# Sink-window attention, cosine FFN and top-1 experts on one core: masks, first pair and routing constants in another order

## The chip, the cores and the metric

One NeuronCore of a Trainium2 chip runs the whole program. It has a tensor engine (PE, with its weight loads as PEld), VectorE (DVE), ScalarE (ACT), GpSimd (POOL) and SyncE (SP); 16 DMA engines move data between HBM and SBUF. The metric is the device time of one execution in microseconds; of several runs the median is given.

## The reference

```python
# attention: q, k, v are 4 x 8 x 768 x 64; 4 sink keys, a window of 128
scores = scale * np.matmul(q, k.transpose(0, 1, 3, 2))
keep = is_sink | in_window            # key < n_sink, or 0 <= row - key < window
scores = np.where(keep, scores, -1e9)
a = softmax(scores); x = a @ v        # -> 3072 tokens x 512
# feed-forward, 512 -> 2048 -> 512
h = x @ w_in; x = (h * np.cos(h)) @ w_out
# eight experts, one per token
logits = x @ w_gate + modality_bias[modality_id]
e_idx = np.argmax(logits, axis=1); gate_w = softmax(logits)[e_idx]
out[mask] = gate_w * (np.maximum(x[mask] @ w1[e], 0.0) @ w2[e])
```

`n_sink` and `window` are inputs that the kernel reads at run time; the weights of the feed-forward layer come as 64-bit floats.

## The kernel before

**Tiling.** Work is cut into eight halves of 384 tokens (one batch element has two). In each half, attention goes by four pairs of heads; then the FFN works on the half as one tile, over 16 blocks of 128 hidden units. The code weaves the FFN of one half into the attention of the next; in the first half there is attention alone, and beside it the conversion of the FFN's weights (`conv_gen`, three raw buffers of 512 KB): a scaled copy on ScalarE (`cv_h`, line 261), bit operations on VectorE, a rounded copy on ScalarE (line 299) and a difference on VectorE.

**One pair of heads** (`attn_front`). Queries and keys are loaded by four DMAs on SyncE (lines 424, 425; every second pair uses other tiles, `ld_x`), transposed on the tensor engine into `pq` and `pk` (lines 444, 454), and evicted by ScalarE into `qT` and `kT` (lines 450, 468); VectorE copies the sink keys. `mid` makes six score tiles `ps` (line 136 through `mm`), takes their masked minimum on VectorE (line 502, writing `Pb` and `mx`; it needs `masks`) and the exponential on ScalarE (line 518). `rest` transposes the probabilities (`pt`, lines 555, 556), multiplies with the values (`po`), scales by the sums (`pf`, a product with the identity matrix `ident`) and writes `xT`. The values' loads are `load_v` (lines 432, 433).

**Set-up** (lines 842 to 943). The two limits are loaded into `rt` (lines 849, 850), converted (`rf`, line 852) and clamped into `lim`. From them come the test `bad` (is the window or the number of sinks beyond what the fast path handles?) and, with two iotas of GpSimd, the three masks. After that stand constants that only the routing of tokens needs, much later: `sides`, `tri`, `ones`, `bias_all`, `tok1`, `e8`, `base`, `inv`, with three loads (`wg`, `mb`, `mid`, lines 916 to 920; `mid` is 3072 items of 8 bytes).

**The general path** (line 160) is a branch that every engine takes part in: it reads `bad_i` into a register (line 943) and jumps over a block that would redo the attention for any limits. It isn't taken here.

**Order of issue.** Each engine works through its own queue in order. The order within it isn't the order of the code: a scheduler draws it up when the program is built, from the code's order, the dependencies and its own costs; the trace shows the result (`cv_h` stands before `qT` on ScalarE, though the code has it behind). An If is one unit to it, but other instructions may be moved past it.

**The expert stage** walks over pages of 256 tokens; a page with more than 128 filled rows takes one arm of an If, others the other (`full`, lines 1330 on). A branch hint, line 1327, tells the tensor engine alone which arm comes.

Of the kernel before, what the change touches and what calls it, by code (L numbers as in the profile page):

```python
# [11 lines left out]
F32 = DT.float32  # L12
# [8 lines left out]
P = 128  # L21
# [35 lines left out]
CONV_A = 0.2  # L57
CONV_LEAD = 8


@with_exitstack
def kernel(
# [92 lines left out]
    def general_attention():  # L155
# [3 lines left out]
        NB = S // P  # L159
        with tc.If(bad_r > 0):  # L160
            def room(tag, n):
# [90 lines left out]
    def conv_out(cpool, f):  # L252
        r = cpool.tile([P, 2 * DM], I32, name="cv_out", tag="cv_raw", bufs=CVB)
        SP.dma_start(out=r, in_=w_out[f * P:(f + 1) * P, :])
        return r

    def conv_bits(cpool, raw):
        w = raw.rearrange("p (n t) -> p n t", t=2)
        lo, hi = w[:, :, 0], w[:, :, 1]
        h = cpool.tile([P, 512], F32, name="cv_h", bufs=2)  # L260
        ACT.activation(out=h, in_=hi.bitcast(F32), func=AF.Copy, scale=REBASE)
        h = h.bitcast(I32)
        a = cpool.tile([P, 512], I32, name="cv_a", bufs=2)
# [131 lines left out]
    def attn_front(hb, pr):  # L395
# [66 lines left out]
        if stack:  # L462
            ACT.activation(out=kT[0][:, 0:nblk, 0:P], in_=pk3[:, 0:nblk, :], func=AF.Copy)
            tt(DVE, kT[1][:, 0:nblk, 0:P], pk3[:, 0:nblk, :], kT[0][:, 0:nblk, 0:P].bitcast(F32), ALU.subtract)
            for i in range(2):
                DVE.tensor_copy(kT[i][:, 0:nblk - 1, P:SEG], ks[:, pr, i:i + 1, :].to_broadcast([P, nblk - 1, NS]))
        else:
            ACT.activation(out=kT[0][:, 0:nblk, 0:P], in_=pk3[:, 0:nblk, :], func=AF.Copy)  # L468
            src = pk3[:, 0:1, 0:NS] if half == 0 else ks[:, pr, 0:1, :]
            DVE.tensor_copy(kT[0][:, 0:nblk - 1, P:SEG], src.to_broadcast([P, nblk - 1, NS]))  # L470
# [394 lines left out]
    win_c = lim[:, 1:2]  # L865
    bad = tmpc.tile([P, 2], F32, name="bad")
    ts(DVE, bad[:, 0:1], ns_c, float(NS), ALU.is_gt)
    ts(DVE, bad[:, 1:2], win_c, float(P), ALU.is_gt)
    tt(DVE, bad[:, 0:1], bad[:, 0:1], bad[:, 1:2], ALU.add)
    ts(DVE, bad[:, 1:2], win_c, 1.0, ALU.is_lt)  # L870
    tt(DVE, bad[:, 0:1], bad[:, 0:1], bad[:, 1:2], ALU.add)
    bad_i = const.tile([P, 1], I32, name="bad_i")
    DVE.tensor_copy(bad_i, bad[:, 0:1])


    iota_i = tmpc.tile([P, NV], I32, name="iota_i")
    POOL.iota(iota_i, pattern=[[1, NV]], base=0, channel_multiplier=0)
    iota_f = const.tile([P, NV], F32, name="iota_f")
    DVE.tensor_copy(iota_f, iota_i)
    prow_i = tmpc.tile([P, 1], I32, name="prow_i")  # L880
    POOL.iota(prow_i, pattern=[[0, 1]], base=0, channel_multiplier=1)
    cols2 = const.tile([P, 2], F32, name="cols2")
    prow, half_pi = cols2[:, 0:1], cols2[:, 1:2]
    DVE.tensor_copy(prow, prow_i)

    masks = const.tile([P, 3, W3], BF16, name="masks")
    rel = tmpc.tile([P, P], F32, name="rel")
    sk = tmpc.tile([P, P], F32, name="sk")
    mw = tmpc.tile([P, P], F32, name="mw")
    ts(DVE, rel, iota_f[:, 0:P], prow, ALU.subtract, -1.0, ALU.mult)  # L890
    ts(DVE, sk, iota_f[:, 0:P], ns_c, ALU.is_lt)
    POOL.memset(masks, 0.0)

    ts(DVE, mw, rel, win_c, ALU.is_lt)
# [8 lines left out]
    DVE.tensor_copy(masks[:, 2, P:SEG], sk[:, 0:NS])  # L903
    ts(DVE, masks, masks, -1.0, ALU.add, -NEG / SCALE, ALU.mult)

    sides = const.tile([P, 2, P], BF16, name="sides")
    ts(DVE, sides[:, 0], rel, 0.0, ALU.is_gt)
    ts(DVE, sides[:, 1], rel, 0.0, ALU.is_le)
    tri = const.tile([P, P], BF16, name="tri")
    ones = const.tile([P, P], BF16, name="ones")  # L910
    ts(DVE, tri, rel, 0.0, ALU.is_lt)
    DVE.memset(ones, 1.0)
    DVE.memset(half_pi, HALF_PI)

    wg = const.tile([P, KD, NE], F32, name="wg")
    SP.dma_start(out=wg, in_=w_gate.rearrange("(c p) e -> p c e", p=P))
    mb = tmpc.tile([P, 2, NE], F32, name="mb")
    SP.dma_start(out=mb, in_=mod_bias.rearrange("(o m) e -> o (m e)", o=1).partition_broadcast(P).squeeze(1).rearrange("p (m e) -> p m e", m=2))
    mid = tmpc.tile([P, NTI, 2], I32, name="mid")
    SP.dma_start(out=mid, in_=modality.rearrange("(t p) w -> p t w", p=P))  # L920
    bias_all = const.tile([P, NTI, NE], F32, name="bias_all")
    btmp = tmpc.tile([P, NTI, NE], F32, name="btmp", tag="iota_i")
    m01 = tmpc.tile([P, NTI, 2], F32, name="m01")
    DVE.tensor_copy(m01[:, :, 1], mid[:, :, 0])
    ts(DVE, m01[:, :, 0], m01[:, :, 1], -1.0, ALU.mult, 1.0, ALU.add)
    b3 = [P, NTI, NE]
    tt(DVE, bias_all, m01[:, :, 0:1].to_broadcast(b3), mb[:, 0:1, :].to_broadcast(b3), ALU.mult)
    tt(DVE, btmp, m01[:, :, 1:2].to_broadcast(b3), mb[:, 1:2, :].to_broadcast(b3), ALU.mult)
    tt(DVE, bias_all, bias_all, btmp, ALU.add)


    tok1 = const.tile([P, NTI], F32, name="tok1")
    ts(DVE, tok1, iota_f[:, 0:NTI], float(P), ALU.mult, 1.0, ALU.add)
    ts(DVE, tok1, tok1, prow, ALU.add)
    e8 = const.tile([P, NE], F32, name="e8")
    ts(DVE, e8, iota_f[:, 0:NE], -1.0, ALU.mult, float(NE), ALU.add)
    base = const.tile([P, NE], F32, name="base")
    DVE.memset(base, 0.0)
    inv = const.tile([P, NV + 2], F32, name="inv")
    DVE.memset(inv, 0.0)  # L940

    tmps.close()
    bad_r = nc.values_load(bad_i[0:1, 0:1], min_val=0, max_val=3)


    next(conv)
    for _ in first:
        pass
    fronts[0, 0][0]()
    mids.add((0, 0))  # L950
    for _ in fronts[0, 0][1]():
        pass
    general_attention()
    conv_done = 1

    def conv_to(n):
        nonlocal conv_done
        while conv_done < n:
            conv_done += 1
            next(conv, None)  # L960

    for n_, _ in enumerate(attn_half(0)):
        conv_to(int(CONV_A * n_))
    def more_wi():
        assert conv_done < 4 * NE1
# [48 lines left out]

    ET = mybir.EngineType
    ALLE = (ET.Pool, ET.Activation, ET.PE, ET.DVE, ET.SP)
# [274 lines left out]
    def run(T):  # L1291
# [102 lines left out]
```

## Time and profile before

| | |
|---|---|
| median of 3 runs | 1143.38 us (1141.84 to 1145.58) |
| the profiled execution | 1143.94 us, of which the span 1142.2 us |
| tensor engine busy | 1103.6 us |
| VectorE busy | 678.3 us |
| ScalarE busy | 602.5 us |
| GpSimd busy | 224.5 us |
| DMA | 113.40 MB, mean 99 GB/s |

The span is the time from the first to the last instruction in the trace; what lies around it is the rest of the measured time. A busy tensor engine is not one at its peak, since matmuls are pipelined. Rows of a timeline give the start in us from the span's start, the length in us, the engine, the line, the operation, what is written from what, and in brackets how long the engine had been idle and what ended that. "SPq" is the issue of a DMA by SyncE, not the transfer.

### The profile page before, as it was taken

How to read it: one execution, taken by the hardware profiler on the slowest of the kernel's cores; microseconds unless marked ns; L12 is line 12 of the kernel's file. 1: busy time of each engine (PE TensorE's matmuls, PEld its weight loads, DVE VectorE, ACT ScalarE, POOL GpSimd, SP SyncE). 2: the span in 40 equal slices, each digit the busy share in tenths (PEclk: the TensorE clock that was granted, in tenths of full speed). 3: DMA queues.
4: the chain of work that ended last, by engine and by line, in shares of the span. 5: the costliest groups of instructions: out<-in, count | busy, mean ns of one | idle time of the engine just before them, and what ended most of it. 6: DMA issues, size and time to landing. Idle time of an engine off the chain costs nothing.

```text
span 1142.2 us, 20840 instructions
## 1 busy us (share of the span) xinstructions
PE 1103.6 (97%) x6624; PEld 928.0 (81%) x6624; DVE 678.3 (59%) x2126; ACT 602.5 (53%) x1239; POOL 224.5 (20%) x273
## 2 busy tenths in 40 slices
PE   5989999999999999999999999999999999999995
PEld 3667777888888878888888879999889998899984
DVE  6778888666876766776676774746742125522210
ACT  5878887656665566665657553434322225422221
POOL 1232224211111111111111111322121211221110
PEclk9999999999999999999999999999999999999998
DMA  6567665422332322323233223633151115111110
GB/s 150 151 197 196 195 195 158 109 73 68 95 74 76 105 72 64 108 70 75 63 104 79 62 75 102 230 93 89 60 203 40 57 58 184 41 58 39 40 43 23
DMA packets 136083, 113.40 MB, mean 99 GB/s; under 512 B 95727, under 2 KB 103919, under 8 KB 135920
## 3 DMA queue, kind: packets, MB, share of 16 engines
q1 hardware_dynamic: 131600, 97.87, 30.3%
q0 software_dynamic: 4320, 13.65, 3.7%
q8 instruction: 66, 1.08, 0.4%
q14 instruction: 97, 0.79, 0.2%
HBM read 151.06 MB, written 19.67 MB: 149 GB/s over the span
## 4 chain that ended last, share of the span: by engine, by line
PE 85%; DVE 5%; DMA 5%; ACT 2%; issue 1%; POOL 1%; SPq 0%; DVEq 0%; POOLq 0%; ACTq 0%
PE hp L136 23%; PE y L626 22%; PE m_h L136 10%; PE m_y L136 10%; PE ps L136 5%; PE po L136 5%; DMA out_dram<-m_ot,m_ids 3%; DMA cv_in<-in_moe_w_in_dram 1%; PE pl L754 1%; PE pq L444 1%; PE pt L546 1%; PE yT L743 1%; PE pk L454 1%; PE m_a L1093 1%; PE mh L136 1%
## 5 line engine op out<-in xcount | busy, mean ns | idle before, releaser
L148 POOL TENSOR_TENSOR g_l<-ch,g_h 128x384 fp32r<-128x384 f32 x128 | 132.4, 1035 | 558.2 <-ACT g_h L698 435.4
L136 PE MATMUL hp<-xT_h,wi_h 128*128 128x384 f32 x512 | 188.3, 368 | 2.7 <-DVE ch L148 2.7
L136 PE MATMUL hp<-xT_h,wi_l 128*128 128x384 f32 x512 | 174.5, 341 | 0.0
L136 PE MATMUL hp<-xT_l,wi_h 128*128 128x384 f32 x512 | 174.0, 340 | 0.0
L626 PE MATMUL y<-wo,g_h 128*128 128x512 f32 x384 | 158.6, 414 | 0.0
L626 PE MATMUL y<-wo_l,g_h 128*128 128x512 f32 x384 | 155.6, 405 | 0.0
L626 PE MATMUL y<-wo,g_l 128*128 128x512 f32 x384 | 154.1, 401 | 0.2 <-POOL g_l L148 0.2
L688 ACT ACTIVATE ch<-ch,cols 128x384 f32<-128x384 f32 x128 | 78.7, 616 | 116.6 <-DVE ch L145 116.0
L136 PE MATMUL m_y<-wi_h,hT 128*128 128x512 f32 x416 | 132.5, 393 | 0.7 <-ACT m_ot L1135 0.6
L145 DVE SCALAR_TENSOR_TENSOR hT<-m_h,hT 128x256 fp32r<-128x256 f32 x88 | 37.3, 424 | 151.0 <-ACTq L1287 102.4
L136 PEld LDWEIGHTS hp<-xT_h,wi_h 128*128 128x128 f32 x512 | 96.7, 189 | 18.1 <-issue 7.2
L142 DVE TENSOR_SCALAR ch<-hp 128x384 int32<-128x384 f32 x128 | 70.9, 554 | 59.1 <-PE hp L136 46.3
L698 ACT ACTIVATE g_h<-ch 128x384 fp32r<-128x384 f32 x128 | 66.4, 520 | 67.8 <-DVE ch L148 46.0
L136 PEld LDWEIGHTS hp<-xT_l,wi_h 128*128 128x128 f32 x512 | 97.0, 189 | 3.7 <-issue 0.2
L136 PEld LDWEIGHTS hp<-xT_h,wi_l 128*128 128x128 f32 x512 | 96.7, 189 | 1.2 <-issue 0.9
L148 DVE TENSOR_TENSOR ch<-ch,hp 128x384 f32<-128x384 f32 x128 | 70.4, 550 | 39.9 <-ACT ch L688 39.5
L136 PEld LDWEIGHTS m_y<-wi_h,hT 128*128 128x128 f32 x416 | 78.1, 188 | 17.0 <-issue 1.0
L518 ACT ACTIVATE Pb<-Pb,mx 128x272 f32<-128x272 f32 (+1 forms) x168 | 82.9, 494 | 10.9 <-DVE mx L502 10.0
L626 PEld LDWEIGHTS y<-wo,g_l 128*128 128x128 f32 x384 | 72.2, 188 | 14.8 <-POOL g_l L148 0.8
L626 PEld LDWEIGHTS y<-wo,g_h 128*128 128x128 f32 x384 | 72.4, 189 | 13.8 <-issue 3.3
L502 DVE CUSTOM_DVE_ANT_0 Pb<-ps,masks 128x272 f32<-128x272 f32 (+1 forms) x168 | 63.7, 411 | 31.7 <-PE ps L136 31.2
L136 PE MATMUL ps<-kT,qT 64*128 64x272 f32 (+1 forms) x504 | 72.6, 350 | 8.9 <-ACT kT L468 7.0
(276 smaller groups left out, 2236.0 us busy)
## 6 DMA issues: line engine op xcount, KB each, us to landing
rw<-in_moe_w_dram SPq DMA_DIRECT2D x112, 512.0 KB
wo_l<-wl_scr SPq DMA_DIRECT2D x122, 256.0 KB
cv_in<-in_moe_w_in_dram SPq DMA_DIRECT2D x16, 512.0 KB
cv_out<-in_moe_w_out_dram SPq DMA_DIRECT2D x16, 512.0 KB
y_scr<-yt SPq DMA_DIRECT2D x24, 256.5 KB
xT_h<-xg_h SPq DMA_DIRECT2D x32, 192.0 KB
xT_l<-xg_l SPq DMA_DIRECT2D x32, 192.0 KB
qn<-in_q_dram SPq DMA_DIRECT2D x56, 96.0 KB
```

What stands on the lines that cost most here:

```text
L136: PE.matmul(o, l, r, start=start, stop=stop)
L142: e.tensor_scalar(out=o, in0=i, scalar1=s1, scalar2=s2, op0=op0, op1=op1)
L145: e.scalar_tensor_tensor(out=o, in0=i0, scalar=s, in1=i1, op0=op0, op1=op1)
L148: e.tensor_tensor(out=o, in0=a, in1=b, op=op)
L444: PE.transpose(pq[:, t * P:(t + 1) * P], qn[:, t].rearrange("p j d -> p (j d)"), ident)
L454: PE.transpose(pk[:, t * P:(t + 1) * P], kn[:, t].rearrange("p j d -> p (j d)"), ident)
L502: DVE.tensor_tensor_reduce(out=Pb[t][j][:, c0:c1], in0=ps[j][:, 0:w], in1=masks[:, min(half * NQ + t, 2), c0:c1], scale=-SCALE, scalar=3.0 ...
L518: ACT.activation(out=Pb[t][j][:, c0:c1], in_=Pb[t][j][:, c0:c1], func=AF.Exp, scale=-1.0, bias=mx[:, i:i + 1], accum_out=sm[:, i:i + 1])
L546: PE.transpose(pt2[:, j * P:(j + 1) * P], Pb[t][j][:, SEG:W3], ident)
L626: i = PE.matmul(o, l, r, start=start, stop=stop)
L688: ACT.activation(out=ch, in_=ch, func=AF.Sin, scale=TWO_PI, bias=half_pi)
L698: ACT.activation(out=gh, in_=ch, func=AF.Copy)
```

## The change

The set-up is put in another order. The limits' DMAs go to ScalarE's queue; iotas and mask fill come first on GpSimd; the masks' instructions on VectorE are tied into one order; the test follows them, with `max` for the additions; the test's register is read there and a branch hint with the label of the general path is placed for four engines. Only then the first pair's loads, transposes and scores stand in the code, VectorE's part behind the masks; between transposes and scores ten products of the identity with itself go into a PSUM bank that nobody reads. The first conversion on ScalarE is tied behind the eviction of the first keys. The router's three loads stand behind the general path, and the router's constants at the twelfth step of the first half's attention. In the expert stage the hint goes to ScalarE and VectorE too. Values computed are the same.

```diff
+RCONST = 12
+WARM = 10
...
-        with tc.If(bad_r > 0):
+        with tc.If(bad_r > 0, preferred_fallthrough_block=True, label="general"):
...
+    nosync = mybir.DependencyInfo(mybir.DependencyClass.NoSync, mybir.DependencyReason.DATA)
+    front_act = []
...
-        ACT.activation(out=h, in_=hi.bitcast(F32), func=AF.Copy, scale=REBASE)
+        i_ = ACT.activation(out=h, in_=hi.bitcast(F32), func=AF.Copy, scale=REBASE)
+        if front_act:
+            tc.add_manual_dep(i_.ins, front_act[-1].ins.name, nosync, reason="behind the first keys")
+            front_act.clear()
...
+            i_ = ACT.activation(out=kT[0][:, 0:nblk, 0:P], in_=pk3[:, 0:nblk, :], func=AF.Copy)
+            if hb == 0 and pr == 0:
+                front_act.append(i_)
...
-    first = attn_front(0, 0)
-    next(first)
-    next(first)
...
-    SP.dma_start(out=rt[:, 0:2], in_=n_sink.partition_broadcast(P).squeeze(1))
-    SP.dma_start(out=rt[:, 2:4], in_=window.partition_broadcast(P).squeeze(1))
+    ACT.dma_start(out=rt[:, 0:2], in_=n_sink.partition_broadcast(P).squeeze(1))
+    ACT.dma_start(out=rt[:, 2:4], in_=window.partition_broadcast(P).squeeze(1))
+
+    iota_i = tmpc.tile([P, NV], I32, name="iota_i")
+    POOL.iota(iota_i, pattern=[[1, NV]], base=0, channel_multiplier=0)
...
+    POOL.memset(masks, 0.0)
+
+    at_ = len(nc.cur_bb.bb.instructions)
...
+    made = DVE.tensor_scalar(out=masks, in0=masks, scalar1=-1.0, scalar2=-NEG / SCALE, op0=ALU.add, op1=ALU.mult)
+    mine = [i_ for i_ in nc.cur_bb.bb.instructions[at_:] if i_.engine == made.ins.engine]
+    for a_, b_ in zip(mine, mine[1:]):
+        tc.add_manual_dep(b_, a_.name, nosync, reason="masks in this order")
+
+    with tc.issue_after(made.ins):
+        bad = tmpc.tile([P, 2], F32, name="bad")
...
+        DVE.tensor_copy(bad_i, bad[:, 0:1])
+    bad_r = nc.values_load(bad_i[0:1, 0:1], min_val=0, max_val=1)
+    ET = mybir.EngineType
+    tc.mark_branch_hint_location("general", hint=bad_r, engines=(ET.PE, ET.Activation, ET.DVE, ET.Pool))
+    with tc.issue_after(made.ins):
+        first = attn_front(0, 0)
+        for _ in first:
+            pass
+        warm = ps_y(0, "warm")
+        for _ in range(WARM):
+            mm(warm[:, 0:P], ident, ident, True, True)
+        mids.add((0, 0))
+        for _ in fronts[0, 0][1]():
+            pass
+        next(conv)
+        fronts[0, 0][0]()
     DVE.memset(half_pi, HALF_PI)
+    general_attention()
+    conv_done = 1
...
     for n_, _ in enumerate(attn_half(0)):
         conv_to(int(CONV_A * n_))
+        if n_ == RCONST:
+                sides = const.tile([P, 2, P], BF16, name="sides")
+                ts(DVE, sides[:, 0], rel, 0.0, ALU.is_gt)
...
+                inv = const.tile([P, NV + 2], F32, name="inv")
+                DVE.memset(inv, 0.0)
+    tmps.close()
...
-                tc.mark_branch_hint_location(f"full{T + 1}", hint=flags[T + 1, "full"], engines=(ET.PE,))
+                tc.mark_branch_hint_location(f"full{T + 1}", hint=flags[T + 1, "full"], engines=(ET.PE, ET.Activation, ET.DVE))
```

## Rows read from the trace of the kernel before

**Rows 1.** The page's busy times: engine, us, share of the span, instructions.

```profile
PE 1103.6 (97%) x6624; PEld 928.0 (81%) x6624; DVE 678.3 (59%) x2126; ACT 602.5 (53%) x1239; POOL 224.5 (20%) x273
```

**Rows 2.** Waits of the tensor engine, 0 to 120 us: total, times, longest.

```profile
PE ps L136 <- ACT kT L468: 7.0, 1, 7.0
PE pq L444 <- DMA qn<-in_q_dram: 4.5, 1, 4.5
PE hp L136 <- DVE ch L148: 2.7, 1, 2.7
```

**Rows 3.** Timeline of the tensor engine: start, us, line, operation, count, idle before.

```profile
5.21 0.88 PE L454 MATMUL pk<-ident,kn 128*128 128x128 f32 x3
...
15.27 3.90 PE L136 MATMUL ps<-kT,qT 64*128 64x272 f32 x8 [1.13 <-DVE mx L502]
19.09 0.90 PE L444 MATMUL pq<-ident,ld_x 128*128 128x128 f32 x3
...
21.81 0.42 PE L555 MATMUL pt<-ident,Pb 128*128 128x128 f32 x1
...
25.22 0.27 PE L555 MATMUL pt<-ident,Pb 128*128 128x128 f32 x1
...
26.03 0.55 PE L454 MATMUL pk<-ident,kn 128*128 128x128 f32 x3
...
29.68 0.94 PE L136 MATMUL pf<-ident,pb_x 128*128 128x128 f32 x6
```

**Rows 4.** Timeline of VectorE (DVE), the same columns.

```profile
1.13 0.17 DVE L912 MEMSET ones<- 128x128 bf16 x1
...
7.01 0.17 DVE L852 CAST rf<-rt 128x4 f32<-128x4 int32 x1 [5.47 <-DMA rt<-in_window_dram]
...
13.14 0.36 DVE L142 TENSOR_SCALAR masks<-masks 128x816 bf16<-128x816 bf16 x1
...
14.18 0.23 DVE L140 TENSOR_SCALAR tok<-tok,cols 128x24 f32<-128x24 f32 x1
...
14.92 0.28 DVE L502 CUSTOM_DVE_ANT_0 Pb<-ps,masks 128x128 f32<-128x128 f32 x1
...
19.71 0.08 DVE L502 DVE_READ_ACCUMULATOR2_ANT mx<- 128x1 f32 x1
...
23.03 0.29 DVE L502 CUSTOM_DVE_ANT_0 pb_x<-ps,masks 128x128 f32<-128x128 f32 x1
...
25.84 0.08 DVE L502 DVE_READ_ACCUMULATOR2_ANT mx<- 128x1 f32 x1
```

**Rows 5.** The chain that ended last, 0 to 110 us: start, us, what.

```profile
11.58 0.66 ACT cv_h L261
...
25.98 0.86 ACT pb_x L518 x3
```

**Rows 6.** Timeline of SyncE's queue (SPq): start and length of each DMA's issue.

```profile
1.78 0.48 SPq L424 DMA_DIRECT2D qn<-in_q_dram  x1
...
3.36 0.43 SPq L850 DMA_DIRECT2D rt<-in_window_dram  x1
...
5.34 2.80 SPq L249 DMA_DIRECT2D cv_in<-in_moe_w_in_dram  x2
...
14.52 0.49 SPq L425 DMA_DIRECT2D ld_x<-in_k_dram  x1
...
21.85 0.68 SPq L425 DMA_DIRECT2D kn<-in_k_dram  x1
```

**Rows 7.** Two stretches: length, busy PE, PEld, DVE, ACT, POOL (instructions), clock, DMA share, GB/s.

```profile
29.00:31.00 2.00, 2.00 (x20) 1.49 (x16) 1.03 (x2) 1.83 (x4) 0.00 (x0) 1.00 0.01 2
60.00:80.00 20.00, 16.87 (x96) 12.70 (x95) 14.65 (x39) 15.10 (x33) 5.68 (x13) 0.91 0.76 228
```

**Rows 8.** The read of the general path's test (line 943) on SyncE.

```profile
L943 SPq TENSOR_LOAD <-bad_i x1: 462/462/462, 9.8 to 9.8; - x1
```

**Rows 9.** Waits of the tensor engine in the expert stage, 820 to 1142 us.

```profile
PE m_h L136 <- ACT m_ot L1135: 1.7, 2, 0.8
```

More of the change, by code (lines that the diff above doesn't have):

```diff
@@ L467, in attn_front @@
         else:
-            ACT.activation(out=kT[0][:, 0:nblk, 0:P], in_=pk3[:, 0:nblk, :], func=AF.Copy)
+            i_ = ACT.activation(out=kT[0][:, 0:nblk, 0:P], in_=pk3[:, 0:nblk, :], func=AF.Copy)
+            if hb == 0 and pr == 0:
+                front_act.append(i_)
             src = pk3[:, 0:1, 0:NS] if half == 0 else ks[:, pr, 0:1, :]
@@ L848 @@
     rt = tmpc.tile([P, 4], I32, name="rt")
-    SP.dma_start(out=rt[:, 0:2], in_=n_sink.partition_broadcast(P).squeeze(1))
-    SP.dma_start(out=rt[:, 2:4], in_=window.partition_broadcast(P).squeeze(1))
+    ACT.dma_start(out=rt[:, 0:2], in_=n_sink.partition_broadcast(P).squeeze(1))
+    ACT.dma_start(out=rt[:, 2:4], in_=window.partition_broadcast(P).squeeze(1))
+    iota_i = tmpc.tile([P, NV], I32, name="iota_i")
+    POOL.iota(iota_i, pattern=[[1, NV]], base=0, channel_multiplier=0)
+    prow_i = tmpc.tile([P, 1], I32, name="prow_i")
+    POOL.iota(prow_i, pattern=[[0, 1]], base=0, channel_multiplier=1)
+    masks = const.tile([P, 3, W3], BF16, name="masks")
+    POOL.memset(masks, 0.0)
+    at_ = len(nc.cur_bb.bb.instructions)
+    iota_f = const.tile([P, NV], F32, name="iota_f")
+    DVE.tensor_copy(iota_f, iota_i)
+    cols2 = const.tile([P, 2], F32, name="cols2")
+    prow, half_pi = cols2[:, 0:1], cols2[:, 1:2]
+    DVE.tensor_copy(prow, prow_i)
+    rel = tmpc.tile([P, P], F32, name="rel")
+    sk = tmpc.tile([P, P], F32, name="sk")
+    mw = tmpc.tile([P, P], F32, name="mw")
+    ts(DVE, rel, iota_f[:, 0:P], prow, ALU.subtract, -1.0, ALU.mult)
     rf = tmpc.tile([P, 4], F32, name="rf")
@@ L865 @@
     win_c = lim[:, 1:2]
[L866 to L890, printed above, removed]
     ts(DVE, sk, iota_f[:, 0:P], ns_c, ALU.is_lt)
-    POOL.memset(masks, 0.0)
     ts(DVE, mw, rel, win_c, ALU.is_lt)
@@ L903 @@
     DVE.tensor_copy(masks[:, 2, P:SEG], sk[:, 0:NS])
[L904 to L912, printed above, removed]
-    DVE.memset(half_pi, HALF_PI)
-    wg = const.tile([P, KD, NE], F32, name="wg")
@@ L916 @@
[L916 to L952, printed above, removed]
+    made = DVE.tensor_scalar(out=masks, in0=masks, scalar1=-1.0, scalar2=-NEG / SCALE, op0=ALU.add, op1=ALU.mult)
@@ new lines @@
+    mine = [i_ for i_ in nc.cur_bb.bb.instructions[at_:] if i_.engine == made.ins.engine]
[3 more added lines that the diff above has]
+        bad = tmpc.tile([P, 2], F32, name="bad")
+        ts(DVE, bad[:, 0:1], ns_c, float(NS), ALU.is_gt)
+        ts(DVE, bad[:, 1:2], win_c, float(P), ALU.is_gt)
+        tt(DVE, bad[:, 0:1], bad[:, 0:1], bad[:, 1:2], ALU.max)
+        ts(DVE, bad[:, 1:2], win_c, 1.0, ALU.is_lt)
+        tt(DVE, bad[:, 0:1], bad[:, 0:1], bad[:, 1:2], ALU.max)
+        bad_i = const.tile([P, 1], I32, name="bad_i")
+        DVE.tensor_copy(bad_i, bad[:, 0:1])
@@ L960, in conv_to @@
             next(conv, None)
+    wg = const.tile([P, KD, NE], F32, name="wg")
+    SP.dma_start(out=wg, in_=w_gate.rearrange("(c p) e -> p c e", p=P))
+    mb = tmpc.tile([P, 2, NE], F32, name="mb")
+    SP.dma_start(out=mb, in_=mod_bias.rearrange("(o m) e -> o (m e)", o=1).partition_broadcast(P).squeeze(1).rearrange("p (m e) -> p m e", m=2))
+    mid = tmpc.tile([P, NTI, 2], I32, name="mid")
+    SP.dma_start(out=mid, in_=modality.rearrange("(t p) w -> p t w", p=P))
     for n_, _ in enumerate(attn_half(0)):
         conv_to(int(CONV_A * n_))
+        if n_ == RCONST:
+                sides = const.tile([P, 2, P], BF16, name="sides")
+                ts(DVE, sides[:, 0], rel, 0.0, ALU.is_gt)
+                ts(DVE, sides[:, 1], rel, 0.0, ALU.is_le)
+                tri = const.tile([P, P], BF16, name="tri")
+                ones = const.tile([P, P], BF16, name="ones")
+                ts(DVE, tri, rel, 0.0, ALU.is_lt)
+                DVE.memset(ones, 1.0)
+                bias_all = const.tile([P, NTI, NE], F32, name="bias_all")
+                btmp = tmpc.tile([P, NTI, NE], F32, name="btmp", tag="iota_i")
+                m01 = tmpc.tile([P, NTI, 2], F32, name="m01")
+                DVE.tensor_copy(m01[:, :, 1], mid[:, :, 0])
+                ts(DVE, m01[:, :, 0], m01[:, :, 1], -1.0, ALU.mult, 1.0, ALU.add)
+                b3 = [P, NTI, NE]
+                tt(DVE, bias_all, m01[:, :, 0:1].to_broadcast(b3), mb[:, 0:1, :].to_broadcast(b3), ALU.mult)
+                tt(DVE, btmp, m01[:, :, 1:2].to_broadcast(b3), mb[:, 1:2, :].to_broadcast(b3), ALU.mult)
+                tt(DVE, bias_all, bias_all, btmp, ALU.add)
+                tok1 = const.tile([P, NTI], F32, name="tok1")
+                ts(DVE, tok1, iota_f[:, 0:NTI], float(P), ALU.mult, 1.0, ALU.add)
+                ts(DVE, tok1, tok1, prow, ALU.add)
+                e8 = const.tile([P, NE], F32, name="e8")
+                ts(DVE, e8, iota_f[:, 0:NE], -1.0, ALU.mult, float(NE), ALU.add)
+                base = const.tile([P, NE], F32, name="base")
+                DVE.memset(base, 0.0)
+                inv = const.tile([P, NV + 2], F32, name="inv")
+                DVE.memset(inv, 0.0)
+    tmps.close()
     def more_wi():
@@ L1012 @@
     att.close()
-    ET = mybir.EngineType
     ALLE = (ET.Pool, ET.Activation, ET.PE, ET.DVE, ET.SP)
```

## The prediction

> **What bounds the kernel now.** I read the page's busy shares first, then the waits of the tensor engine, then the timelines of its first 36 us, then the branch's own line. Over the whole span the array is busy 97% of the time [rows 1], so only an edit that fills its idle time or shortens its own work can move the end. The idle time stands nearly all in one place: of the waits up to 120 us, 7.0 us are for the first keys (kT) and 4.5 us for the first queries' DMA and 2.7 us come at one later place [rows 2]. The front is where this change works, so a gain has to come from the 11.5 us of waits there, or from the clock.
>
> The clock is the second thing to see. The granted-clock column reads 1.00 from the start, but durations say otherwise: a 128x128 transpose takes 0.42 us at 21.81 and 0.27 us at 25.22 [rows 3]. [...] The six first-pair scores' maxima take from 14.92 to 19.79 (4.87 us), those of the second pair 23.03 to 25.92 (2.89 us) [rows 4].
>
> Why so late? ScalarE is in order, and its first conversion (cv_h) stands ahead of the eviction of the first queries; it starts at 11.58, when the weights' DMA has landed [rows 5]. VectorE gets the two limits at 7.01, has the masks ready at 13.50, then still does conversions before the first maximum at 14.92 [rows 4].
>
> **The change, part by part.** The sum is made on the profiled execution, 1143.94 us (a span of 1142.2 and 1.74 around it), 0.56 above the median of the three runs, 1143.38; I subtract from the median.
>
> *Limits and masks.* The two limits' DMAs leave SyncE's queue, where the second is issued at 3.36 to 3.79 and used at 7.01, 3.2 us later [rows 4, 6]; the last queries took 2.2 us from the end of issue (2.26) to use (4.45) [rows 2, 6]. As first instructions of ScalarE's queue they would be issued by about 1.7, so used at 3.9 to 4.9; I take 4.9, by the limits' own delay (2 us more would change nothing, since the array binds, below). From the limits' first conversion at 7.01 to the end of the masks at 13.50 it is 6.5 us [rows 4]; six test instructions in between, some 1.2, move behind the masks, and router constants, copies of keys and a wait for the keys, nine pieces of some 2.0, go away. Masks: 4.9 + 3.3 = 8.2, instead of 13.50. The fixed order among the masks' instructions adds a wait only for GpSimd's two iotas, long done by then. cv_h is pinned behind the eviction of the first keys, near 6.6; behind it only conversions wait, and its data would not be there before 7, so this costs nothing.
>
> *Ten products.* No row shows them. The nearest is the 128x128 product with `ident` (pf), 3 in 0.94 us at the upper clock: 0.3 us each, so 0.6 at the lower [rows 3]. Ten cost 3 to 6 us of the array. If they follow the key transposes, which end at 6.1 [rows 3], the array is free at 9.1 to 12.1; I take 10.6, half at either clock. That is later than the masks, so they are not free: the first maximum comes at about 11.0, 3.9 us earlier than 14.92, where the masks alone would allow 8.4. In return the clock is up for the scores: 2.89 instead of 4.87 us for the six maxima. Last maximum 13.9 instead of 19.79, 5.9 earlier. If they are put ahead of the query transposes (the code's order isn't the issue order: cv_h comes after the key transposes in the code) it comes to the same within 1 us, since the array idles until 4.45.
>
> [...] Row first: before the durations halve, the array has done nothing but transposes from 19.09 to 22.45, behind the scores [rows 3]. [...]
>
> *Loads of the next pairs.* SyncE issues one DMA per 0.51 us (seven from 1.78 to 5.34). Now, the second pair's last keys are issued at 14.52 to 15.01 and the third pair's at 21.85 to 22.53 [rows 6]. After: four first loads, three weights, four values, the three router loads (now behind the If in the code, but loads are moved past it today: the second pair's stand before the branch) and then the second pair's four: 18 x 0.5 + 0.75 = 9.8, plus 1.8 for the DMA behind `mid`, which now takes 2.3 instead of 0.5 us to issue (the row of 5.34, two in 2.80), plus 0.8 around the test's read: 12.4, 2.6 us earlier. Usable 2.2 later, at 14.6, against the second keys' transposes at 19.8, behind the queries' of 19.09 [rows 3]: 5.2 earlier. The third pair's keys were there at about 22.53 + 2.2 = 24.7, used at 26.03 [rows 3]; 2.6 earlier they allow 22.1: **3.9 us earlier**. The array works in order, so the smallest of 5.9, 5.2 and 3.9 is what gets through: -3.9. Bounds: +0.7 (the second rival) and -5.9. What stood behind it gets later no more: the next loads on SyncE wait for the first pair's output product, which is earlier by then.
>
> *Behind that place* ScalarE's evictions and exponentials stand in the chain from 25.5 to 31.2, five pieces of 2.7 us in all (the longest is shown [rows 5]); with the second pair 5.9 ahead and the third 3.9, part is hidden: 0 to -2.7, I take -0.8.
>
> *Router constants.* Fourteen instructions between 1.13 and 14.41 (the first and the last are shown [rows 4]), 3.1 us in all on VectorE, of which some 2.6 lie between limits and first maximum today (their absence is counted above). They come back at the twelfth step of the first half, around 28 us, where VectorE is busy 1.03 of 2 us [rows 7]: two such stretches take them in. Without that cover 3.1; I take +0.4.
>
> *Test and hint.* Today no wait of the array is put down to the branch [rows 2]; reading the test takes a sequencer 0.46 us [rows 8], which is what an earlier read can save or cost. It is read on every engine early now, and on VectorE six test instructions (1.2 us) stand between masks and first maximum, in the shadow of the ten products; queued behind that read are the first maxima, and the array waits for those. -0.6 to +0.8, I take -0.3.
>
> *Hints in the expert stage.* The array waits 1.7 us in two places there, for evictions, not for the branch [rows 9]. 0 to -1; I take 0.
>
> Sum: -3.9 - 0.8 + 0.4 - 0.3 = -4.6; 1143.38 - 4.6 = **1138.8 us**. About 0.3% (3.4 us) is what a measurement of this kernel can tell from no change.
>
> **The rivals.**
> *All of the front is carried.* If the router loads stand behind the second pair's loads in the queue, or `mid` holds nothing up, the loads cease to bind and 5.9 plus parts of the evictions come through; the later wait of 2.7 us may go with it, whose stretch shows a clock of 0.91, 1.8 us lost in 20 [rows 2, 7]. -6 to -9: 1134.4 to 1137.4.
> *The loads bind.* The test stays as early in SyncE's queue as now (after eleven DMAs; its read starts at 9.8 [rows 8], and the test won't be ready before 9.5). Then three router loads with their 1.8 and the second pair's four come behind it: 10.3 + 3.5 + 1.8 = 15.6, 0.7 later than now. Only the work pulled ahead remains: the first pair's transposes and output, some 2 us. 0 to -3.4: 1140 to 1143.4.
> *Slower: the array falls idle twice.* The same queue order with values still behind the test (two more, 16.7) delays the third pair's loads by 1.7; the array, done with the first pair at 14, waits four us for the second pair's queries and drops to the lower clock, as it did after 2.7 us of waiting [rows 2, 7], for 1.8 more. +1.7 + 1.8 = +3.5: 1146.9. It decides if the second pair's queries land after about 17.
> *The change doesn't do what it says:* the order is drawn up by the scheduler, which may put the constants or the test ahead of the masks all the same; then only the eviction order is won and the first maximum comes at about 13: within -2 of now.
>
> **How the numbers follow.** Forecast (-3.4 to -6) 0.42; all carried 0.20; loads bind or no effect 0.30; slower by the queue 0.08. Faster by over 0.3%: 0.40 + 0.20 = 0.60; within: 0.32; slower: 0.08. The range leaves out the deepest part of the second case and the last: 1134.0 to 1144.0.
>
> **What would show it.** The profile after should show the first maximum (line 502's read-out) at 9.5 to 11.5 and the sixth by 14.5; a transpose of 0.27 us before 13; ScalarE's first eviction near 5.5, ahead of cv_h; ten `warm` products behind the key transposes; the second pair's transposes at 14 to 15 and the third pair's keys' at about 22; the first row of the FFN earlier by 4 to 5 us, and the same distance kept up to the end. The prediction is wrong if SyncE reads the test before the router loads, if the clock falls between 13 and 18, or if the distance won at 30 us is gone at 130.

## The result and the profile after

| | kernel before | changed kernel |
|---|---|---|
| median (runs) | 1145.81 us (6) | 1157.26 us (6), 1153.81 to 1159.44 |
| ratio, 95% interval | 1 | 1.0102 [1.0085, 1.0119] |
| profiled execution, its span | 1143.94, 1142.2 us | 1156.15, 1154.4 us |

The change costs 11.5 us where 4.6 less were forecast. The first thing to read is the page's line of busy times:

```profile
PE 1113.9 (96%) x6644; PEld 936.0 (81%) x6644; DVE 680.1 (59%) x2126; ACT 606.3 (53%) x1241; POOL 225.5 (20%) x273
```

Against [rows 1] the tensor engine is busy 10.3 us longer, of 12.2 us by which the span grew. So hardly any idle time was added, and none was won: the array does the same work (and ten products) more slowly. The second thing is where the distance arises. The same piece of work, by its number among the records of the trace, starts at:

| piece of work | before | after | difference |
|---|---|---|---|
| first output product `po` | 28.23 | 32.77 | +4.5 |
| 49th record of `po` | 48.25 | 52.21 | +4.0 |
| 97th record of the FFN's `hp` | 123.5 | 127.4 | +3.9 |
| 289th record of `hp` | 220.3 | 230.0 | +9.7 |
| first `m_h` of the expert stage | 841.7 | 851.3 | +9.6 |
| 553rd record of `m_h` | 981.5 | 994.0 | +12.4 |

Three places: the front (+4.0), 50 to 230 us (+5.7, all of it behind 123), and one page of the expert stage (+2.9).

**The front.** Waits of the tensor engine, 0 to 40 us (total, times, longest), then VectorE's timeline and the tensor engine's, columns as in [rows 3]:

```profile
PE pq L452 <- DMA qn<-in_q_dram: 5.8, 1, 5.8
PE ps L138 <- DVE bad_i L916: 3.3, 1, 3.3
PE pt L566 <- DVEq L162: 1.1, 1, 1.1
```

```profile
8.84 0.37 DVE L903 TENSOR_SCALAR masks<-masks 128x816 bf16<-128x816 bf16 x1
...
9.37 0.16 DVE L150 TENSOR_TENSOR bad<-bad 128x1 f32<-128x1 f32 x1
13.80 0.18 DVE L962 CAST m<-mid 128x24 f32<-128x24 int32 x1 [4.28 <-DMA mid<-in_moe_modality_id_dram]
...
14.45 0.18 DVE L480 COPY kT<-pk 128x32 f32<-128x32 f32 x1
14.56 0.15 DVE L916 CAST bad_i<-bad 128x1 int32<-128x1 f32 x1
...
15.54 0.29 DVE L512 CUSTOM_DVE_ANT_0 Pb<-ps,masks 128x128 f32<-128x128 f32 x1 [0.56 <-PE ps L138]
...
20.27 0.08 DVE L512 DVE_READ_ACCUMULATOR2_ANT mx<- 128x1 f32 x1
```

```profile
5.77 0.88 PE L452 MATMUL pq<-ident,qn 128*128 128x128 f32 x3 [5.77 <-DMA qn<-in_q_dram]
...
7.07 4.02 PE L138 MATMUL warm<-ident 128*128 128x128 f32 x20
11.02 0.49 PE L138 MATMUL ps<-kT,qT 64*128 64x128 f32 x2
14.78 0.76 PE L138 MATMUL ps<-kT,qT 64*128 64x128 f32 x2 [3.27 <-DVE bad_i L916]
...
30.07 0.42 PE L566 MATMUL pt<-ident,pb_x 128*128 128x128 f32 x1
...
32.34 0.50 PE L452 MATMUL pq<-ident,ld_x 128*128 128x128 f32 x3
```

The masks are ready at 9.21 instead of 13.50. Four instructions later the scheduler has put a conversion of the router, the cast of `mid`, into the middle of the test: it stands at the twelfth step in the code and before the first maximum in VectorE's queue. SyncE's queue shows why it is late (the issue of `mid` and of the second pair's last keys):

```profile
9.70 0.37 SPq L947 DMA_DIRECT2D mid<-in_moe_modality_id_dram  x1
...
13.59 0.49 SPq L433 DMA_DIRECT2D ld_x<-in_k_dram  x1
```

So VectorE stands still for 4.28 us, with the masks made and the first score done. Behind the cast are the copy of the sink keys (L480), the test and the first maximum, which comes at 15.54 instead of 14.92 [rows 4].

The stretches (length, busy time of PE, PEld, DVE, ACT and POOL, granted clock, DMA share, GB/s) show the clock:

```profile
0.00:15.00 15.00, 5.96 (x29) 5.71 (x30) 7.39 (x46) 2.82 (x4) 2.47 (x11) 0.96 0.74 169
15.00:30.00 15.00, 13.82 (x50) 8.91 (x51) 10.33 (x40) 11.64 (x36) 1.53 (x4) 0.50 0.64 161
30.00:45.00 15.00, 13.57 (x92) 8.81 (x91) 9.66 (x41) 11.53 (x35) 4.10 (x8) 0.97 0.43 113
```

It rises at 10.5, during the products, falls at 13.9, after the array has stood still from 11.5, and is at 0.50 until 30.9; in the kernel before, the transposes turn from 0.42 to 0.27 us between 22 and 25 [rows 3]. The clock column reads 1.00 up to 10.5 all the same, as it does up to 22.6 in the kernel before, which is why the first stretch shows 0.96. That the clock is low before 10.5 is read from the durations: three transposes take 0.88 us at 5.77 and 0.50 at 32.34.

**The expert stage.** ScalarE, 975 to 983 us, waits 3.06 us for nothing that the profile shows ("issue"); the array then waits 1.3 us for its result:

```profile
976.21 0.28 ACT L1138 ACTIVATE hT<-m_y 128x128 fp32r<-128x128 f32 x1 [0.40 <-DVE hT L150]
979.55 0.28 ACT L1138 ACTIVATE hT<-m_y 128x128 fp32r<-128x128 f32 x1 [3.06 <-issue]
```

### The profile page after: what moved, and what is told of

Same layout as the page of the kernel before. It is cut to its first block, busy times and chain, and to the rows that moved or that the text cites. A ratio compares the mean times of both kernels' runs of the same rounds, so it can differ in the third digit from the quotient of the medians.

```text
span 1154.4 us, 20919 instructions
## 1 busy us (share of the span) xinstructions
PE 1113.9 (96%) x6644; PEld 936.0 (81%) x6644; DVE 680.1 (59%) x2126; ACT 606.3 (53%) x1241; POOL 225.5 (20%) x273
## 5 line engine op out<-in xcount | busy, mean ns | idle before, releaser
L138 PE MATMUL hp<-xT_h,wi_l 128*128 128x384 f32 x512 | 174.3, 340 | 0.0
L528 ACT ACTIVATE Pb<-Pb,mx 128x272 f32<-128x272 f32 (+1 forms) x168 | 82.9, 494 | 11.1 <-DVE mx L512 10.4
L138 PE MATMUL m_y<-wi_l,hT 128*128 128x512 f32 x208 | 81.0, 389 | 0.0
```

The source lines that it names most:

```text
L138: PE.matmul(o, l, r, start=start, stop=stop)
L528: ACT.activation(out=Pb[t][j][:, c0:c1], in_=Pb[t][j][:, c0:c1], func=AF.Exp, scale=-1.0, bias=mx[:, i:i + 1], accum_out=sm[:, i:i + 1])
```

## The experiments

The first theory: the cast of `mid` in VectorE's queue costs the front and, by the idle array, the clock. Rivals: the ten products; the early read of the test by all engines; the order of the later work; the hints in the expert stage. "Constants" are the router's; ratios are to the kernel before, timed beside each run.

### e1: the constants where the change puts them

```diff
         if n_ == RCONST:
+            last = [i_ for i_ in nc.cur_bb.bb.instructions if i_.engine == made.ins.engine][-1]
+            with tc.issue_after(last):
```

> The changed kernel, with the router's constants held behind the last VectorE instruction that stands ahead of them in the code, so that they come at the twelfth step as the change says. Theory (the cast of `mid`, drawn up ahead of the test, holds VectorE from 9.5 to 13.8 and with it the read of the test on every engine, so that the array falls idle and the clock drops): test ready by about 10 instead of 14.6, no wait of the tensor engine for bad_i over 0.5 us, first Pb at 11.2 instead of 15.5, granted clock of 15 to 30 us near 1 instead of 0.50; 1149 to 1152 us, that is 5 to 8 less than the changed kernel. Rival (the front loses by the ten products or by the early read itself): the wait for bad_i goes, but the first keys of the FFN come less than 1.5 us earlier; 1155 to 1158. Rival (the loss comes later, from another order of the work between 130 and 230 us): the front gains 4.5, but the end moves by less than 2; 1155 to 1157.

Measured: 1160.53 us, ratio 1.0124 [1.0107, 1.0141], not less than the changed kernel. The cast is gone from the front and the first maximum's read-out ends at 11.9 (forecast: about 11.0). But the tensor engine's waits, 0 to 40 us, are now:

```profile
PE pq L452 <- DMA qn<-in_q_dram: 5.7, 1, 5.7
PE pt L566 <- DVEq L162: 3.2, 1, 3.2
PE pq L452 <- DMA ld_x<-in_q_dram: 3.0, 1, 3.0
```

The scheduler has put the second pair's query transposes between the first pair's scores, and their data land at 15.7; then 3.2 us are lost behind the branch. The sixth maximum ends at 20.7. The cast did hold VectorE, but what it held would have waited anyway: half of the theory falls, and none of the three ranges holds.

### e2: no ten products

```diff
-WARM = 10
+WARM = 0
```

> The changed kernel without the ten products. Theory (test behind the cast of `mid`): VectorE waits until 13.8 as before, the first score is still held to about 14.7, and the array is only idle for longer ahead of it; 1156 to 1159, within 1.5 us of the changed kernel. Rival (the ten products cost the loss at the front, 4 us of the array): 1153 or less.

1153.77 us, 1.0068 [1.0051, 1.0085]: 3.9 us less than the changed kernel (1.0102 - 1.0068), more than the theory allows and less than the rival asks for. The front is as the theory has it (the array waits 4.6 us for VectorE until 15.6, and the first `po` comes only 1.3 us earlier, at 31.5), so the time isn't won there. From the 49th `po` to the 289th `hp` it takes 172.7 us, as the kernel before (172.1), where the changed kernel takes 177.8. The scheduler counts the products: without them the queues have another order from the second score on.

### e3 and e12: the hints of the expert stage alone

```diff
-                tc.mark_branch_hint_location(f"full{T + 1}", hint=flags[T + 1, "full"], engines=(ET.PE,))
+                tc.mark_branch_hint_location(f"full{T + 1}", hint=flags[T + 1, "full"], engines=(ET.PE, ET.Activation, ET.DVE))
```

> The kernel before, with the hint of the expert stage given to ScalarE and VectorE as well as to the tensor engine, and nothing else. Theory (the 2.85 us that arise between 945 and 994 us are the price of the two hints): 1148.3 to 1149.2, with the distance to the kernel before zero until 900 us and arising at the page that is not full. Rival (they come from the later arrival of that stage and its transfers): within 0.7 us of the kernel before.

1150.63 us, 1.0038 [1.0023, 1.0053], so 4.4 us, somewhat more than the theory's 2.85. In its profile 3.5 arise between 959 and 979 us and 1.5 up to the first `po`, from the clock (below). In e12 ScalarE alone is hinted:

> The kernel before, with the hint of the expert stage given to ScalarE too, but not to VectorE. In e3, with both, ScalarE and VectorE stand still together for 3.0 us at about 969, the tensor engine 1.9 us at 960 instead of 0.8, and the distance to the kernel before grows by 3.5 us between 959 and 979. [...] Rival (only VectorE's hint costs): the distance grows by less than 0.5 us there.

The distance grows by 3.1 us in the same place (one run, 1151.14). ScalarE's timeline, e3 and then e12:

```profile
972.29 0.28 ACT L1123 ACTIVATE hT<-m_y 128x128 fp32r<-128x128 f32 x1 [2.74 <-issue]
```

```profile
974.31 0.28 ACT L1123 ACTIVATE hT<-m_y 128x128 fp32r<-128x128 f32 x1 [2.78 <-issue]
```

The kernel before has no "issue" wait of ScalarE there. So the hint to ScalarE is enough; VectorE stands still only because it waits for ScalarE's result (2.7 us in e3, 2.8 in e12). The other profiles agree: from the 440th to the 553rd record of `m_h` the distance to the kernel before grows by 2.9 to 3.5 us in all seven kernels in which ScalarE has the hint, and by -0.3 to +0.9 in the seven others.

e3 and e12 show something else. Their first 900 us are the same queues in the same order as the kernel before, and still the first `po` comes at 29.7 and 30.6 instead of 28.2. The clock rises at 26.9 and 29.6 instead of 22.6, and the same twelve records take 2.28 us in the kernel before and 3.51 in e3 (both from the tensor engine's timeline):

```profile
22.45 2.28 PE L136 MATMUL ps<-kT,qT 64*128 64x128 f32 x12
```

```profile
22.28 3.51 PE L136 MATMUL ps<-kT,qT 64*128 64x128 f32 x12
```

The profile on which the prediction was made had its clock up early; in these three profiles the front varies by 2.4 us without any change, so up to that much of the +4.0 above is the early clock of the kernel before.

### e4: no hint for the general path

```diff
-    tc.mark_branch_hint_location("general", hint=bad_r, engines=(ET.PE, ET.Activation, ET.DVE, ET.Pool))
```

> The changed kernel without the branch hint for the general path: each engine then reads the test only where it comes to the branch. Theory (VectorE's own wait for `mid` is what holds): the tensor engine no longer waits for bad_i ahead of its second score, but the first maximum still can't come before 13.8; first Pb at 14.2 to 15, 1154 to 1157, 0 to 2 us less than the changed kernel. Rival (the early read by all engines is what costs): the first Pb near 11.5 and 1150 to 1153.

1156.07 us, 1.0090 [1.0073, 1.0107], 1.4 less than the changed kernel. That is within the theory's 0 to 2, but the two intervals overlap, so a gain isn't shown. The wait of the tensor engine, which should have gone, stays, although it now reads the test only at 18.8 (VectorE's timeline, then the tensor engine's):

```profile
14.77 0.18 DVE L480 COPY kT<-pk 128x32 f32<-128x32 f32 x1
```

```profile
15.10 0.76 PE L138 MATMUL ps<-kT,qT 64*128 64x128 f32 x2 [3.49 <-DVE bad_i L916]
```

In both kernels the second score starts 0.15 us after the end of L480 (14.95 and 15.10 here, 14.63 and 14.78 in the changed kernel), the last reader of `pk`. The array's own read of the test comes 3.7 us later in e4, so it isn't what holds the score. The profile names `bad_i` because it came last; by these times the array waits for VectorE's copy behind the cast.

### e5, e6, e9: the new order without products and without the expert stage's new hints

e5 is e1 with WARM = 0 and the tensor engine's hint alone. e6 moves the router's loads behind the second pair's and ties that pair's transposes behind the first pair's scores; e9 takes the general path's hint out of e6.

```diff
+        if n_ == 0:
+            lsp = [i_ for i_ in nc.cur_bb.bb.instructions if i_.engine == ET.SP][-1]
+            with tc.issue_after(lsp):
+                ... the loads of wg, mb, mid ...
...
+            tc.add_manual_dep(i_.ins, scored[0], nosync, reason="behind the first pair's scores")
```

> The changed kernel with the router's constants held at the twelfth step, without the ten products, and with the hint of the expert stage for the tensor engine alone: the new order of the set-up by itself. Theory (the idle time of the array ahead of the first output product is set by when the second pair's loads land and by what follows the branch, so that it is moved and not won): idle time up to the first po of 13 to 15 us, as in the kernel before (13.5), clock up by 23 to 28 us; 1145 to 1149. Rival (the early masks do carry once products and hints are gone): idle time of 10 us or less and 1140 to 1143.

> The kernel of e5 with two more edits: the router's three loads stand on SyncE behind the second pair's queries and keys instead of ahead of them, and the second pair's transposes stand on the tensor engine behind the first pair's scores. Theory (the loads bind): the second pair's queries are issued near 7.5 instead of 11 and land by 12.5 instead of 15.7, the wait for them falls below 0.5 us, and the time is 2 to 4 us less than e5. Rival (the wait only goes over to the branch or to the evictions on ScalarE, which wait for the conversion's data): within 1 us of e5.

> The kernel of e6 without the branch hint for the general path, so that each engine reads the test where it comes to the branch. In e1, e5, e6 and e8 VectorE's first instruction behind the branch comes 3.0 us after it (in the kernel before and in e4, without a hint, 0.6 to 0.7), and the array waits 3.2 us for it. Theory (the hint costs these 3 us): VectorE goes on within 1 us of the branch, the array's wait there falls below 1.2 us, the clock rises earlier than the 29.0 of e6, and the time is 2 to 5 us less than e6: 1146 to 1149. Rival (the place of the branch in the new order costs them, hint or not): the wait of about 3 us stays, and the time is within 1 us of e6.

e5: 1151.27 us, 1.0034 [1.0020, 1.0049]; up to the first `po` there are 14.6 us without a record of the tensor engine (13.5 in the kernel before), so the idle time is moved and not won, as the theory says; the time is above its range, and the clock rises only at 31.2 where 23 to 28 was expected. e6: 1151.04, 1.0038 [1.0024, 1.0052]; the wait for the second pair's queries is gone, and the time is the same, as the rival says. But it isn't the same by the rival's mechanism: the first `po` comes 3.0 us earlier than in e5 (31.2 against 34.2), and of a distance of 4.7 us at the 49th `po` 1.9 is left at the 289th `hp`. e9: 1152.42, 1.0048 [1.0033, 1.0063]; the 3 us behind the branch stay without the hint: the theory falls. In e6 the largest wait after the first queries is

```profile
PE pt L574 <- DVEq L162: 3.2, 1, 3.2
```

### e13: what the 3 us behind the branch hang on

```diff
+    pad = tmpc.tile([P, 1], F32, name="pad")
+    for _ in range(14):
+        DVE.memset(pad, 0.0)
```

> The kernel of e9 with fourteen memsets of one column ahead of the first instruction of the masks, in VectorE's idle time before 2.3 us; the order of all queues is that of e9 otherwise. Theory (the number of VectorE's instructions ahead of the branch decides, so that 72 instead of 58 take the stall away): VectorE goes on within 0.9 us of the branch instead of 3.0, the array's wait there falls from 3.8 to about 1.5, the first po comes 1.5 to 3 us earlier than 29.8; 1149 to 1151 if what follows keeps the distance. Rival (it is something else in that order): the 3.0 us stay, and the time is within 1 us of e9.

VectorE's timeline behind the branch, e9 and then e13:

```profile
21.10 0.69 DVE L147 SCALAR_TENSOR_TENSOR cv_a<-cv_in,cv_a 128x512 int32<-128x512 int32 x1 [3.61 <-DVEq L162]
```

```profile
18.65 0.69 DVE L147 SCALAR_TENSOR_TENSOR cv_a<-cv_in,cv_a 128x512 int32<-128x512 int32 x1 [1.23 <-DVEq L162]
```

The theory holds for the branch: with the order unchanged, fourteen idle memsets take 2.4 us off VectorE's idle time there, and the array's wait falls from 3.8 to 1.4. It also holds across the runs: with 52 to 59 instructions of VectorE ahead of the branch (as the trace records them, the sequencer's included) its next comes 2.9 to 3.0 us behind it, with 61 and more 0.5 to 1.2. What VectorE waits for behind the branch the profile doesn't show. The traces also have queues named `instruction`. From 5 to 17.9 us, just ahead of the branch, they are (transfers, MB, share of the DMA engines) in e9 and then in e13:

```profile
q8 instruction: 1, 0.02, 0.5%
```

```profile
q8 instruction: 1, 0.02, 0.5%
q14 instruction: 1, 0.01, 0.2%
```

The transfer that the memsets add starts at 12.87. In all ten profiles with the short wait a transfer of 8 KB on q14 starts 2.2 us or more before VectorE's branch ends; in the five with the long wait none does, from 0 us on, by more than 0.4. So the short wait and such a transfer come together in these fifteen profiles; which engine the transfer serves isn't recorded, and that the one causes the other was not shown.

The gain is given back at once: the first `po` is at 29.8 in both; the clock rises at 27.6 in e13 and at 24.5 in e9. 1150.61, 1.0030 [1.0017, 1.0043], against 1.0048, which is no difference beyond the intervals.

### e7, e8, e14: products and the clock

e7 is e1 with thirty products and the tensor engine's hint alone; e8 is e1 with ten transposes in place of the products; e14 is the kernel before with the ten products behind the first key transposes, all five queues otherwise in the same order.

> The changed kernel with the constants held at the twelfth step, the hint for the tensor engine alone, and thirty products instead of ten, so that the array has work until about 15.5 us, when the second pair's queries land. Theory (with ten products the clock rises near 10.5 and falls again because the array then stands still): with thirty it rises near 10.5 and doesn't fall again before 30; a transpose of the second pair takes 0.27 us; the first po comes 3 to 5 us earlier than with ten products and the constants held (35.9); 1150 to 1154. Rival (the clock falls near 14 however busy the array is): transposes of 0.42 us after 16, first po at 35 or later, 1156 to 1159.

> The kernel of e1 with ten transposes of the identity in place of the ten products. If transposes count for the clock as products do, the clock rises while they run or right behind them, within 1.5 us of the 10.7 of e1, and falls again near 14. If they don't count, the clock stays at the lower level past 20 us, as in the run without products. Time 1155 to 1162 in both cases.

> The kernel before with the ten products behind the first pair's key transposes, and nothing else; the order of all five queues is that of the kernel before otherwise. The array is idle there from 6.1 to 13.05, so the products (4.0 us) are hidden. Theory (they raise the clock, which falls again because the array stands still from about 10.5 to 13.05): it rises near 10 and falls near 14, the scores run at the lower level, and the next rise comes no earlier than the 22.6 to 29.6 seen for the front of the kernel before; 1146 to 1150, 0 to 3 us more than the kernel before. Rival (the products are worth it where the array isn't kept waiting): the clock stays up from 10 on, six maxima in 2.9 instead of 4.9 us, first po near 26 instead of 28.2; 1142 to 1145. Second rival (products cost nothing and bring nothing): the clock as without them, within 1 us of the kernel before.

Stretches of e7, e8 and e14, cut where the clock changes (columns as above):

```profile
11.50:21.70 10.20, 8.39 (x64) 6.76 (x64) 7.73 (x24) 5.83 (x18) 0.00 (x0) 1.00 0.62 106
21.70:28.50 6.80, 6.80 (x30) 5.16 (x28) 5.63 (x32) 6.08 (x19) 1.11 (x4) 0.50 0.53 130
```

```profile
9.90:13.40 3.50, 1.53 (x6) 0.88 (x6) 2.06 (x10) 3.04 (x9) 0.00 (x0) 0.99 1.05 83
13.40:27.00 13.60, 8.10 (x29) 4.91 (x30) 5.08 (x19) 5.60 (x18) 1.24 (x4) 0.50 0.54 131
```

```profile
9.10:12.50 3.40, 0.73 (x7) 0.54 (x5) 3.38 (x23) 0.85 (x2) 0.00 (x0) 1.00 1.00 310
12.50:29.60 17.10, 15.04 (x53) 10.83 (x54) 12.44 (x51) 12.50 (x37) 1.08 (x4) 0.50 0.64 158
```

e7, 1152.02 us (1.0043 [1.0026, 1.0060]): with products until 16.2 the clock stays up to 21.7 and falls after the waits for the second pair's queries (0.6 us) and behind the branch (1.1). So it didn't fall near 14, as the rival has it, but it fell before 30, against the theory. First `po` 30.6 instead of 35.9. The whole is no faster for it: e5, the same kernel without any product, took 1151.27. e14, 1148.43 us (1.0010 [1.0000, 1.0020]): the products themselves are hidden, the clock is up while the array waits for the keys (busy 0.73 of 3.40 us) and down from 12.5, before the scores come at 13.1. Alone they cost at most 2.3 us and bring nothing. e8 (one run, 1161.79): the clock rises with the ten transposes as with the products, at 9.9 against 10.7 in e1; with neither (e5) it rises at 31.2.

### e11: the order alone

The changed kernel with WARM = 0, no hint for the general path and the tensor engine's hint alone in the expert stage.

> The changed kernel without the ten products, without the hint for the general path and with the hint of the expert stage for the tensor engine alone: what is left is the new order of the set-up, as the scheduler draws it up, with the cast of `mid` ahead of the test. If the parts add up (e2: products 3.4, e3: hints of the expert stage 3.5 to 4, e4: hint of the general path about 1, of 11.6 in all), 1148.5 to 1151. Rival (the order itself is worth something, and the parts overlap): 1146 or less.

1150.13 us, 1.0028 [1.0014, 1.0042], as the parts added up. In its profile the array is busy 1109.6 us, 6.0 more than in [rows 1], and the span is 6.1 longer: its idle time is the same to 0.1 us. It has the lower clock until 31.9 instead of 22.6, and for 6.8 us more near 120, where the kernel before has 3.4 near 67. The parts, each from its own pair of ratios, give 3.2 (order) + 3.9 (products) + 1.4 (hint of the general path) + 4.4 (hints of the expert stage) = 12.9 us; 11.7 were measured, which agrees within their intervals of some 2 us each. Of the four, the 1.4 isn't clear of noise.

## Why the prediction was wrong, point by point

*Limits and masks.* Mostly right: the limits are used at 4.97 (forecast 4.9), the masks are ready at 9.2 (8.2).

*Ten products.* Size right: 4.02 us (3 to 6), array free at 11.1 (10.6). That a product takes twice as long at the lower clock, 0.6 us against 0.3, was the author's estimate; the clock column later showed that clock as 0.50, and at it five of the products took 2.34 us from 7.07, so 0.47 each. What they were for was wrong: "in return the clock is up for the scores" failed, since the array stood still behind them: for 3.27 us between the first and the second score in the changed kernel, and before the first score in e14.

*Test and hint,* "in the shadow of the ten products", and *router constants,* which "come back at the twelfth step". This is the step that failed first. The test wasn't alone between masks and first maximum: the scheduler put the cast of `mid` there, 4.28 us. The prediction had this as its last rival, priced within -2 us; the mechanism came, at a price of the other sign, because the constants were priced by their work on VectorE (3.1 us for all fourteen; the cast takes 0.18) and not by the load that the cast waits for. The hint was given -0.6 to +0.8; without it the time is 1.4 less (e4), which isn't clear of noise, and the branch is no faster with it: VectorE goes on 1.2 us behind it, in e4 0.6.

*First maximum at 11.0, sixth at 13.9.* e1 has the first at 11.9 and the sixth at 20.7. So even with the constants where they were thought to be, the next step fails: between the first pair's scores stand the second pair's transposes, in order, with data that land at 15.7 (14.6 was forecast for the pair's keys). The loads bind, as the second rival says, but not by its mechanism: SyncE reads the test at 14.7, behind these loads and not ahead of them. The last load of the pair's keys is issued by 14.1 where 12.4 was forecast; SyncE's waits on the way are put down to the landing of the weights (1.0 us ahead of `mid`, 1.1 behind it), where the sum had one stall of 1.8 behind `mid`. And "the smallest of 5.9, 5.2 and 3.9 gets through" took three gains in one queue for independent of the order in it.

*The clock.* The prediction named its own end: "if the clock falls between 13 and 18". It fell at 13.9. The slower rival (the array falls idle twice, the clock drops) is nearest in mechanism: price +3.5, measured +4.0 in the front. It was tied to the second pair's queries landing after 17; they landed before 16, and the idle time came from VectorE's queue instead, so that the prices are close is luck.

*Behind that place.* The forecast assumed that the distance of 30 us is kept to the end. It grew by 5.7 between 50 and 230 us. From the 49th `po` to the 289th `hp`, runs with the order of the kernel before take 172.1 to 174.3 us (before, e3, e12, e14), e2, e5 and e11 172.7 to 173.2, the changed kernel and e4 177.8 and 175.7, e6, e9 and e13 176.0 to 177.5, e1, e7 and e8 179.3 to 182.4. Part of that is the clock: a dip of 3.4 us at a clock of 0.50 is some 1.7 us of work lost, and without the dips the first seven take 169.3 to 170.9 us and the other eight 174.0 to 175.8. So some 4 us go with the order that the scheduler draws up for the later work after a small change in front.

In the changed kernel they arise between the 161st and the 289th `hp`. There the array has the same number of records of each tile in both kernels and takes 63.0 us before, 68.8 after. Before, it has no wait over 0.1 us there; in the changed kernel its waits in that stretch are:

```profile
PE pt L566 <- POOL Pb L144: 1.2, 2, 0.8
PE pt L565 <- POOL Pb L144: 0.6, 1, 0.6
PE pt L565 <- DVE qT L150: 0.2, 1, 0.2
```

GpSimd scales the probabilities, and the array comes to some of them too early: 2.0 of the 5.8 us are these waits, 1.7 are the clock dip at 181, and the rest is spread over the products. e13 has 67.3 us there, with 2.1 of such waits and no dip; e11 63.1 with none. Two more table loads on ScalarE go with the slower orders (103 in all eight, 101 in the first seven, 1.28 us each; the pages' x1241 against x1239), but they lie between 60 and 110 us, ahead of that stretch. Which instruction makes GpSimd late was not settled.

The later order decides over the front too: in e6, e7, e9 and e13 the 49th `po` comes at 49.2 to 50.8 us, where the three profiles with the front of the kernel before have 48.3 to 50.7. These four are not behind at 50 us; what they lose, they lose in the later order.

*Hints in the expert stage,* "0 to -1; I take 0". A term put at nothing that is +4.4 by the times (e3), 2.9 to 3.5 by the profiles. A loss was excluded without a reason; the waits of [rows 9] showed that there was nothing to gain, not that there was nothing to lose.

*Transposes and the clock.* The row that the prediction gives, with nothing but transposes from 19.09 to 22.45 ahead of the rise at 22.6, has a like in e8: with only transposes on the array from 5.76 to 9.41 the clock rose at 9.9.

*The base.* 1143.38 was the median of three runs; beside the later runs the same kernel has medians of 1145.81 to 1147.24. The bound "0.7 later than now" of the second rival is 0.6 by its own figures (15.6 against 15.01), which changes nothing.

No run beat the kernel before.

## What to carry to other kernels

Idle time at the start was set here by the last of several late things (loads, evictions, a branch, another engine's queue). With one taken away, the array waited for the next: 7.0 us for the first keys in the kernel before, 3.3 for VectorE's queue in the changed kernel, 3.0 for the second pair's queries and 3.2 behind the branch in e1. So a forecast has to follow the whole queue of each engine up to the first piece of work that isn't late, and to check the order that the scheduler really draws up. A piece of set-up that depended on a late load held its engine's whole queue until the load landed, for 4.28 us here: hold it back by a dependency, not by its place in the code. What is won in front can be lost again in the order that the scheduler then draws up for the later work (some 4 us here), so compare the same piece of work well behind the change. Filling an idle array with products brought nothing where a gap followed them (e14, ratio 1.0010), and the hint to ScalarE, which had no "issue" wait there without it, cost 2.9 to 3.5 us by the profiles.

## What the runs showed of the hardware

- The time at which the clock rose wasn't fixed by the work ahead of it: 22.6, 26.9 and 29.6 us in three profiles with the same queues (before, e3, e12), 2.4 us of time by the first `po`.
- VectorE's first instruction behind the branch of the general path came 2.9 us after it in e9 and 0.5 us after it in e13, and fourteen memsets ahead of the branch made the difference.
- With the expert stage's branch hint ScalarE stood still for 2.74 us in e3, 2.78 in e12 and 3.06 in the changed kernel, for nothing that the profile shows; without it, in the kernel before, it had no such wait there.
- The first queries were used at 5.7 to 6.1 us in every kernel with the new order, at 4.5 to 4.7 in the others. The first of their DMAs is issued at 0.75 us in both; behind them the weights' loads are issued from 2.84 instead of 5.34. Whether that delays the queries was not tried.
